# Attention and two expert layers on one core: the order of all instructions taken from a list schedule written in the source

## The chip, the core and the metric

The kernel runs on one core of a Trainium2 chip. A core has a matrix engine (TensorE, PE in the profile), a vector engine (VectorE, DVE), an activation engine (ScalarE, ACT), a general engine (GpSimd, POOL), and a queue on SyncE (SP) from which this kernel starts all its DMA transfers. Each engine issues its own instructions in a fixed order. Semaphores order them across engines. The metric is the device time of one execution in microseconds (us), the median of several.

## What is computed

The reference, cut to what matters (B, H, S, D = 4, 8, 576, 64; 2304 tokens):

```
scores = q @ k.T / sqrt(D)          # heads 0-3: local mask of 32, heads 4-7: strided mask of 32
x = softmax(scores) @ v             # (2304, 512)
h = x @ w_in                        # 512 -> 2048
g = (a0 + a1 h + a2 h^2 + a3 h^3) / (1 + |b0||h| + |b1|h^2 + 1e-6)
x = g @ w_out                       # 2048 -> 512
h = x @ w_in2                       # 512 -> 1024
u = h * softmax(h); ln = (u - mean) / sqrt(var + 1e-6) * g_ln
out = ln @ w_out2                   # 1024 -> 512
```

## The kernel before

All large products are made with three f16 matmuls, from a high and a low f16 part of each operand. The weights arrive as 64-bit words, so each is converted first: `w_conv` unpacks 1024 columns of words with three VectorE instructions (L151 to L153) and squares them on ScalarE (L159), `w_scales` adds the squares over partitions on TensorE (L84) and makes a power-of-two scale, and `w_split` writes the high part on ScalarE (L184) and the low part on VectorE (L185). `w_in` ("wi") and `w_out` ("wo") have eight granules each. `w_in2` and `w_out2` are converted later, in `w2_work`, with the parts made on ScalarE and GpSimd (L212 to L214).

Attention is cut into 12 units for each of the four batches: scores into a PSUM bank (L291, L292), maximum (L318), exponential (L334), normalisation on GpSimd (L343), transposition on TensorE (L353), product with v (L383), and two evacuations into the f16 blocks `xs` (L414, L422).

The expert layers run over nine blocks of 256 tokens. A block has eight groups of 256 hidden columns, and a step n handles one group: `mm_h` (24 matmuls, L535 to L537) fills one of two "h" banks, five steps later `mm_y` (24 matmuls, L612 to L614) consumes the group's result. Between them a group takes ScalarE (L543, L546, L569, L574, L596), GpSimd (L552, L556, L600) and VectorE (L560, L564, L578, L582, L586). The "h" bank is held until L586, since the reciprocal is written back into it. From step 24 on the second expert layer follows, one tile of 128 tokens for each four steps: `mm_in2` (L645 to L647), its softmax and norm, two transposing DMAs (L713, L714), `mm_out2` (L723 to L725) and `out_evac` (L730).

Order before: the source traces every operation with a priority (`prio`, `p_step`), and the framework's scheduler, which simulates a timeline, picks the order in which each engine issues and which buffer of a ring a tile gets. Attention of batch 0 has the priorities 1000 to 6500, all eight `w_conv("wi")` and their splits 10000 to 12100, step n `40000 + 2000 n`, the "wo" granules those of steps 0 to 7, the `w2_work` of step n those of step n + 2.

Of the kernel before, what the change touches and what calls it, by code (L numbers as in the profile page):

```python
# [7 lines left out]

F32 = mybir.dt.float32
F16 = mybir.dt.float16  # L10
BF16 = mybir.dt.bfloat16
# [25 lines left out]
EXPM = 0x7F800000  # L37


@with_exitstack  # L40
def kernel(ctx: ExitStack, tc: tile.TileContext, qk, v, w_in, w_out, ab, w_in2, w_out2, gln, out):
    nc = tc.nc
    PE, ACT, DVE, POOL, SP = nc.tensor, nc.scalar, nc.vector, nc.gpsimd, nc.sync

    const = ctx.enter_context(tc.tile_pool(name="const", bufs=1))
    wts = ctx.enter_context(tc.tile_pool(name="wts", bufs=1))
    big = ctx.enter_context(tc.tile_pool(name="big", bufs=1))
    tiny = ctx.enter_context(tc.tile_pool(name="tiny", bufs=2))
    ps = ctx.enter_context(tc.tile_pool(name="ps", bufs=1, space=PSUM))

    wi_h = wts.tile([128, KD, DFF], F16, name="wi_h")
# [18 lines left out]
    gs_t = const.tile([128, KF2], F32, name="gs_t")  # L70
    gm2 = const.tile([128, 1], F32, name="gm2")

    def psum(tag, shape=(128, 512), bufs=1):
        return ps.tile(list(shape), F32, tag=tag, name=f"ps_{tag}", bufs=bufs)

    def t1(name, n=1, bufs=2):
        return tiny.tile([128, n], F32, tag=name, name=name, bufs=bufs)

    def ew(name, bufs, shape=(128, 512), dt=F32):
        return big.tile(list(shape), dt, tag=name, name=name, bufs=bufs)  # L80

    def sum_over_partitions(x):
        t = psum("a", bufs=2)[:, 0:x.shape[1]]
# [79 lines left out]
    def w_scales(name, g0, n):  # L163
        sg = sum_over_partitions(ssq[name][:, g0:g0 + n])
        p, s = pat[name][:, g0:g0 + n], scl[name][:, g0:g0 + n]
        DVE.tensor_scalar(p.bitcast(I32), sg.bitcast(I32), 1, EXPM, op0=ALU.logical_shift_right, op1=ALU.bitwise_and)
        DVE.tensor_scalar(s.bitcast(I32), p.bitcast(I32), -1.0, float(EXPM - (51 << 23)), op0=ALU.mult, op1=ALU.add)
# [74 lines left out]
        qk_t[b, p] = t  # L242

    def load_vl(b):
        t = big.tile([128, NLB, 4, D], F32, tag="vl", name="vl", bufs=1)
        SP.dma_start(out=t, in_=v[b, :, 0:NLB])
        vl_t[b] = t

    def load_vs(b):
        t = big.tile([128, NSG, 4, D], F32, tag="vs", name="vs", bufs=1)  # L250
        SP.dma_start(out=t, in_=v[b, :, NLB:NVB])
        vs_t[b] = t

# [182 lines left out]
    def x_scale(i):  # L436
        key = k = blk_key(i)
        if key not in xkey:
            m = vmax[key]
            p = const.tile([128, 1], F32, name=f"xp{k}")  # L440
            s = const.tile([128, 1], F32, name=f"xsc{k}")
            mg = t1("mg")
            DVE.tensor_scalar(mg, m, 2.0 ** -60, None, op0=ALU.add)
            pow2(mg, p, s, 13)
            xkey[key] = (m, p, s)
        xm[i], xpw[i], xsc[i] = xkey[key]
        xs[i] = big.tile([128, 2, KD, TB], F16, tag="xs", name="xs", bufs=4)

    def x_tail(b):
        i = ((b + 1) * S - 1) // TB  # L450
# [280 lines left out]
        SP.dma_start(out=out[t * 128:(t + 1) * 128, :], in_=ot)  # L731


    def prio(p):
        tc.cur_priority = p

    LY = 5
    NSTEP = NB * NG
    M2S = 24
    NT2 = NT // 128  # L740
    P_STEP = 2000
    P0 = 40000

    def p_step(n):
        return P0 + int(n * P_STEP)

    prio(0)
    for t in qk_buf:
        qk_zero(t)
    load_qk(0, 0)  # L750
# [10 lines left out]
    for g in range(3, 8):  # L761
        w_load("wi", g)

    make_identity(nc, ident)
    DVE.memset(ones_f, 1.0)
    for t in sm_buf:
        POOL.memset(t, 1e-9)
# [11 lines left out]
    POOL.tensor_copy(mask_b[0:LQ, 0, 0:LW], mask_l0)  # L779
    POOL.tensor_copy(mask_b[0:LQ, 1, 0:LW], mask_l)  # L780
    POOL.tensor_copy(mask_b[0:126, 2, 0:126].rearrange("p (r t) -> p r t", t=TPR), mask_s)
    ACT.preload_act_table_set("natural_log_exp_and_others")
    ACT.activation(aba, ab_t, AF.Abs)

    v_max(0)
    x_scale(0)
    x_scale(1)
    for u in range(12):
        prio(1000 + 500 * u)
        attn_scores2(0, u)  # L790
        attn_softmax(0, u)
        attn_exp(0, u)
        attn_norm(0, u)
        attn_tp(0, u, "a")
        attn_tpe(0, u)
        attn_pv(0, u, "a")
        attn_xhi(0, u)
        attn_xlo(0, u)
    for g in range(8):
        prio(10000 + 300 * g)  # L800
        w_conv("wi", g)
    for g0 in range(0, 8, 2):
        prio(10000 + 300 * g0)
        w_scales("wi", g0, 2)
        for g in range(g0, g0 + 2):
            prio(10000 + 300 * g)
            w_split("wi", g)
    prio(900)
    w_pmax("wi")
    g_scale(0)  # L810
    gsc[1] = gsc[0]
    prio(20000)
    for g in range(4):
        w_load("wo", g)
    load_qk(1, 0)
# [21 lines left out]
    def step(n):  # L837
        if n == 49:
            x_scale(NB - 1)
            g_scale(NB - 1)  # L840
            x_tail(B - 1)
        un, up, upp = units.get(n), units.get(n - 1), units.get(n - 2)
        hg, h1, h2, hm, hy = grp(n), grp(n - 1), grp(n - 2), grp(n - 3), grp(n - LY)
        if un and un[1] == 0:
            b = un[0]
            v_max(b)
            for j in range((b * S) // TB, ((b + 1) * S - 1) // TB):
                x_scale(j)
                g_scale(j)
            x_tail(b - 1)  # L850
        m = n - M2S
        t, sub = divmod(m, 4) if m >= 0 else (-9, 0)
        t_in = t if 0 <= t < NT2 else None
        t_pr = t - 1 if 0 <= t - 1 < NT2 else None
        t_out = t - 2 if 0 <= t - 2 < NT2 else None

        do(un, attn_scores1, *(un or ()))
        do(t_in is not None and sub == 2, m_max, t_in)
        do(upp, attn_xhi, *(upp or ()))
        do(h2, a_ln, *(h2 or ()))  # L860
        do(t_in is not None and sub == 2, m_exp, t_in)
        do(h2, a_ex, *(h2 or ()))
        do(h1, a_abs, *(h1 or ()))
        do(upp, attn_xlo, *(upp or ()))
        do(h1, v_q1, *(h1 or ()))
        do(h2, v_t, *(h2 or ()))
        do(h1, v_p2, *(h1 or ()))
        do(h2, v_rn, *(h2 or ()))
        do(h1, v_p3, *(h1 or ()))
        do(h2, v_g, *(h2 or ()))  # L870
        do(h1, p_qm, *(h1 or ()))
        do(un, attn_softmax, *(un or ()))
        if hy:
            mm_y(*hy, 0)
            mm_y(*hy, 1)
        do(hg, mm_h, *(hg or ()))
        do(up, attn_tp, *(up + ("a",) if up else ()))
        if sub < 2 and t_in is not None:
            if n >= NSTEP + LY:
                prio(p_step(n - 4))  # L880
            mm_in2(t_in, sub)
            prio(p_step(n + 0.5))
        if sub >= 2 and t_out is not None:
            mm_out2(t_out, sub - 2)
        do(up, attn_tpe, *(up or ()))
        do(up, attn_pv, *(up + ("a",) if up else ()))
        do(hm, a_hi, *(hm or ()))
        do(hm, p_lo, *(hm or ()))
        do(un, attn_exp, *(un or ()))
        if t_in is not None and sub == 2:  # L890
            m_u(t_in)
        if t_in is not None and sub == 3:
            m_sq(t_in)
            m_var(t_in)
            m_rs(t_in)
        if t_pr is not None and sub == 0:
            m_nw(t_pr)
            m_v(t_pr)
            m_hi(t_pr)
        if t_pr is not None and sub == 1:  # L900
            m_lo(t_pr)
        do(un, attn_norm, *(un or ()))
        if hy and hy[1] == NG - 1:
            y_scale(hy[0])
            y_evac(hy[0])
            y_evac2(hy[0])
        if t_out is not None and sub == 3:
            out_evac(t_out)
        if un:
            b, u = un  # L910
            if u == 3:
                load_qk(b, 2)
            if u == 6:
                load_qk(b, 3)
            if b < B - 1:
                if u == 7:
                    load_vl(b + 1)
                if u == 9:
                    load_qk(b + 1, 0)
                if u == 11:  # L920
                    load_qk(b + 1, 1)
        if up and up[1] == 11 and up[0] < B - 1:
            load_vs(up[0] + 1)

    def wo_work(g):
        w_conv("wo", g)
        if g + 4 < 8:
            w_load("wo", g + 4)
        if g % 2 == 2 - 1:
            w_scales("wo", g + 1 - 2, 2)  # L930
            for j in range(g + 1 - 2, g + 1):
                prio(p_step(j))
                w_split("wo", j)
        if g == 7:
            w_pmax("wo")
            for j in range(2):
                sl = slice(64 * j, 64 * j + 64)
                POOL.tensor_copy(cwo[sl, :], inv["wo"][sl, j::2])
# [18 lines left out]
    for n in range(M2S + 4 * (NT2 + 2)):  # L957
        if 0 <= n < 4:
            for g in (2 * n, 2 * n + 1):
                prio(p_step(g))  # L960
                wo_work(g)
        prio(p_step(n + 2))
        w2_work(n)
        prio(p_step(n))
        if n >= M2S and (n - M2S) % 8 == 0 and (n - M2S) // 8 < NB:
            y_scale2((n - M2S) // 8)
        step(n)


def _layout(q, k, v):  # L970
# [53 lines left out]
```

## Time and profile before

| what | value |
|---|---|
| timed executions | 793.4, 796.77, 797.81 us; median 796.77 us |
| span of the profiled execution, first to last instruction | 790.5 us |
| what lies around the span, against the median | 6.3 us |
| TensorE busy | 705.6 us (89%), mean granted clock 0.935 |
| VectorE, ScalarE, GpSimd busy | 570.7, 481.6, 329.0 us |
| chain that ended last | TensorE 70%, VectorE 14%, DMA 5%, ScalarE 5% |

The profile is a separate execution from the three timed ones, and its own time is known only as its span. A granted clock of 1.00 is TensorE's upper level. Records of matmuls overlap: the starts of successive ones tell their pace.

### The profile page before, as it was taken

The numbers are of one execution on the slowest core, as the hardware profiler recorded it, in microseconds if no ns is written. First come the engines' busy times: TensorE is split into PE (matmuls) and PEld (weight loads), VectorE is DVE, ScalarE is ACT, GpSimd is POOL, SyncE is SP. The second block draws the span as 40 slices with busy tenths as digits, with TensorE's granted clock in tenths as the row PEclk, the third lists the DMA queues.
The fourth block names the chain that finished last, engine by engine and source line by source line (L and its number), as shares of the span: only waits on it lengthen the run. The fifth ranks groups of instructions, "written<-read, shape, count | busy, mean of one in ns | idle before, by whom it ended". The sixth has DMA issues, their size and how long they took to land.

```text
span 790.5 us, 14385 instructions
## 1 busy us (share of the span) xinstructions
PE 705.6 (89%) x5406; PEld 534.3 (68%) x5406; DVE 570.7 (72%) x1194; ACT 481.6 (61%) x1143; POOL 329.0 (42%) x312
## 2 busy tenths in 40 slices
PE   4777226999987798999999999999999999999997
PEld 4665115887874687687878786777777777766443
DVE  4889999778869875787977575866657657654562
ACT  2776547766784777876766676746556556543442
POOL 2322425646467547754544434434343434330000
PEclk8665557999999999999999999999999999999999
DMA  9994700153231411122111201011022010111134
GB/s 256 321 257 141 196 18 1 33 161 103 72 102 55 138 34 41 33 54 66 33 41 33 41 2 41 2 41 41 1 41 39 4 41 16 25 41 40 41 80 106
DMA packets 68100, 55.97 MB, mean 71 GB/s; under 512 B 39616, under 2 KB 56000, under 8 KB 67520
## 3 DMA queue, kind: packets, MB, share of 16 engines
q1 hardware_dynamic: 68032, 55.07, 26.8%
q8 instruction: 42, 0.69, 0.4%
q14 instruction: 26, 0.21, 0.1%
HBM read 40.90 MB, written 4.72 MB: 58 GB/s over the span
## 4 chain that ended last, share of the span: by engine, by line
PE 70%; DVE 14%; DMA 5%; ACT 5%; issue 4%; POOL 2%; SPq 1%; ACTq 0%; DVEq 0%; POOLq 0%
PE ps_h L535 7%; PE ps_y L613 7%; PE ps_y L614 7%; PE ps_y L612 7%; PE ps_h L537 7%; PE ps_h L536 7%; PE ps_h L647 3%; PE ps_h L646 3%; PE ps_h L645 3%; PE ps_a L292 3%; PE ps_a L725 3%; PE ps_a L723 3%; PE ps_a L724 3%; PE ps_a L383 3%; DMA wi_h<-in_w_in_dram 2%
## 5 line engine op out<-in xcount | busy, mean ns | idle before, releaser
L535 PE MATMUL ps_h<-xs,wi_h 128*128 128x256 f16 x576 | 161.1, 280 | 25.9 <-DVE p L586 25.8
L536 PE MATMUL ps_h<-xs,wi_h 128*128 128x256 f16 x576 | 161.0, 279 | 0.0
L537 PE MATMUL ps_h<-xs,wi_l 128*128 128x256 f16 x576 | 160.5, 279 | 0.0
L613 PE MATMUL ps_y<-gtb,wo_h 128*128 128x256 f16 x448 | 122.2, 273 | 0.7 <-POOL gtb L600 0.7
L612 PE MATMUL ps_y<-gtb,wo_h 128*128 128x256 f16 x448 | 122.2, 273 | 0.6 <-DVE ysb L628 0.6
L614 PE MATMUL ps_y<-gtb,wo_l 128*128 128x256 f16 x448 | 122.2, 273 | 0.0
L600 POOL TENSOR_TENSOR gtb<-p,gtb 128x512 f16<-128x512 f32 x56 | 66.0, 1178 | 119.5 <-ACT gtb L596 119.5
L552 POOL TENSOR_SCALAR q<-A,aba 128x512 f32<-128x512 f32 x72 | 62.7, 870 | 105.3 <-ACT A L543 105.1
L556 POOL TENSOR_TENSOR q<-q,A 128x512 f32<-128x512 f32 x72 | 99.1, 1377 | 5.3
L560 DVE TENSOR_TENSOR p<-p,ps_h 128x512 f32<-128x512 f32 x72 | 49.2, 683 | 48.3 <-ACT p L546 46.3
L569 ACT ACTIVATE L<-q 128x512 f32<-128x512 f32 x72 | 45.4, 630 | 63.4 <-POOL q L556 63.2
L578 DVE SCALAR_TENSOR_TENSOR q<-q,ps_h 128x512 f32<-128x512 f32 x72 | 49.0, 681 | 41.7 <-ACT ps_h L574 41.2
L535 PEld LDWEIGHTS <-wi_h 128*128 128x128 f16 x576 | 58.0, 101 | 31.0 <-DVE p L586 21.9
L543 ACT ACTIVATE A<-ps_h,ih 128x512 f32<-128x512 f32 x72 | 49.1, 682 | 35.0 <-PE ps_h L537 35.0
L536 PEld LDWEIGHTS <-wi_h 128*128 128x128 f16 x576 | 57.7, 100 | 14.3 <-issue 5.8
L343 POOL TENSOR_TENSOR e<-e,arc 96x508 f32<-96x508 f32 (+3 forms) x36 | 38.9, 1081 | 62.6 <-DVE arc L342 41.6
L612 PEld LDWEIGHTS <-wo_h 128*128 128x128 f16 x576 | 56.5, 98 | 11.1 <-DVE ysb L628 0.9
L537 PEld LDWEIGHTS <-wi_l 128*128 128x128 f16 x576 | 57.7, 100 | 8.2
L613 PEld LDWEIGHTS <-wo_h 128*128 128x128 f16 x576 | 56.5, 98 | 9.9 <-issue 0.2
L596 ACT ACTIVATE gtb<-p 128x512 f16<-128x512 f32 x56 | 35.5, 633 | 44.2 <-DVE p L586 44.1
L614 PEld LDWEIGHTS <-wo_l 128*128 128x128 f16 x576 | 56.4, 98 | 7.6 <-issue 1.0
L334 ACT ACTIVATE e<-ps_a,amx 96x127 f32<-96x127 f32 (+2 forms) x132 | 45.6, 358 | 17.4 <-DVE amx L318 13.7
(331 smaller groups left out, 1811.7 us busy)
## 6 DMA issues: line engine op xcount, KB each, us to landing
qkb<-in_qk_dram SPq DMA_DIRECT2D x28, 304.0 KB, 4.6
out_dram<-ot SPq DMA_DIRECT2D x18, 256.0 KB, 2.5
wo_l<-in_w_out_dram SPq DMA_DIRECT2D x4, 1024.0 KB, 5.7
wo_h<-in_w_out_dram SPq DMA_DIRECT2D x4, 1024.0 KB, 5.4
vl<-in_v_dram SPq DMA_DIRECT2D x4, 768.0 KB, 5.9
wi_h<-in_w_in_dram SPq DMA_DIRECT2D x3, 1024.0 KB, 6.7
wi_l<-in_w_in_dram SPq DMA_DIRECT2D x3, 1024.0 KB, 6.6
wo_h<-in_w_in_dram SPq DMA_DIRECT2D x3, 1024.0 KB, 18.2
```

Of the source, the lines that this page charges most:

```text
L535: PE.matmul(o, lhsT=wi_h[:, k, f:f + 128], rhs=xs[i][:, 0, k, :], start=(k == 0), stop=False)
L536: PE.matmul(o, lhsT=wi_h[:, k, f:f + 128], rhs=xs[i][:, 1, k, :], start=False, stop=False)
L537: PE.matmul(o, lhsT=wi_l[:, k, f:f + 128], rhs=xs[i][:, 0, k, :], start=False, stop=(k == KD - 1))
L543: ACT.activation(A, t, AF.Abs, scale=gsc[i]["ih"][:, g:g + 1])
L552: POOL.tensor_scalar(w["q"], w["A"], aba[:, 5:6], aba[:, 4:5], op0=ALU.mult, op1=ALU.add)
L556: POOL.tensor_tensor(w["q"], w["q"], w["A"], op=ALU.mult)
L560: DVE.tensor_tensor(w["p"], w["p"], hp[i, g], op=ALU.mult)
L578: DVE.scalar_tensor_tensor(w["q"], w["q"], EPS_D, w["r"], op0=ALU.add, op1=ALU.mult)
L600: POOL.tensor_tensor(t[:, :, 1, :], gw.pop((i, g))["p"].rearrange("p (c t) -> p c t", t=TB), t[:, :, 0, :], op=ALU.subtract)
L612: PE.matmul(o, lhsT=wo_h[:, f, w], rhs=gg[:, c, 0, :], start=(f == 0 and d % 2 == 0), stop=False, skip_group_check=True)
L613: PE.matmul(o, lhsT=wo_h[:, f, w], rhs=gg[:, c, 1, :], start=False, stop=False, skip_group_check=True)
L614: PE.matmul(o, lhsT=wo_l[:, f, w], rhs=gg[:, c, 0, :], start=False, stop=(f == KF - 1), skip_group_check=True)
```

## The change

Every call on an engine is recorded first (`Order.record`), with its inputs and outputs as regions of fixed buffers, instead of being traced into the framework. The rings of buffers keep their sizes (two "h" banks, two "a" banks, one pair for "y", one for "h2", two T, one ws, and so on), but which one a value gets is chosen by the list schedule, and the values of a ring are given buffers strictly in the order of the source. Small one-column tiles rotate over six places instead of two. `Order.run` estimates the duration of each instruction, works out due times backward from the last one, and places one instruction after another: of those that can begin within 0.2 us of the earliest, the one that is due first. `Order.emit` issues them in that order in a block in which the framework adds semaphores but does not reorder. The priorities go. "wi" is converted in pairs: conversion, scales and split of granules 0 and 1 stand in the source before attention unit 4, the next pairs before units 6, 8 and 10.

```diff
+    def cost(self, op):
...
+        if op.eng == "PE":
+            f32 = op.ins[-1][1].dtype == F32
+            op.t = max(0.03, size(out) / 2400 * ((3.6 if op.call == "transpose" or out.shape[0] > 64 else 1.8) if f32 else 1))
+        elif op.eng == "ACT":
+            op.t = 0.08 + n * 0.00088 + (0.05 if psum else 0) + (0.09 if "accum_out" in op.k else 0)
...
+        elif op.eng == "DVE":
...
+            fast = not two and not psum and op.call == "tensor_scalar"
+            op.t = 0.07 + n / (1900 if fast else 960) + (0.08 if "accum_out" in op.k else 0)
...
+            op.port = n >= 8 and (len(sb) >= 2 if two else fast)
+        elif op.eng == "POOL":
...
+            op.t = 0.1 + n * (0.002 if h else 0.0022 if two else 0.00125 if op.call == "tensor_scalar" else 0.001)
...
+            op.port = bool(ins)
...
+    def run(self):
...
+        LAG = dict(PE=0.25, ACT=0.15, DVE=0.13, POOL=0.1, SP=0.0)
+        EARLY, PEARLY = 0.3, 1.5
...
+        def begin(op):
+            x = max(free[op.eng], op.ready)
+            if op.port:
+                x = max(x, port)
+            for v in op.values:
+                if v.home is None:
+                    f = [max(cells.get(c, 0.0) for c in h) for h, _ in v.homes]
+                    x = max(x, min(f)) if v.queue[0] is v else BUSY
+            return x
...
+                t, d, i = min((x for x in c if x[0] <= t + SLACK), key=lambda x: x[1:])
...
+            if op.eng == "PE":
+                heat = min(3.4, max(0.0, heat - max(0.0, t - free["PE"])) + d)
+                warm = heat > 3.3 or warm and heat > 1.5
+                d = d if warm else 2 * d
...
+                o.ready = max(o.ready, end + (0.0 if o.eng == op.eng == "PE" else 0.06 if o.eng == op.eng else LAG[op.eng] + (PEARLY if o.eng == "PE" else EARLY)))
...
     def ew(name, bufs, shape=(128, 512), dt=F32):
-        return big.tile(list(shape), dt, tag=name, name=name, bufs=bufs)
+        return View(Value(rings[name], shape, dt))
...
+    def wi_pair(g0):
+        for g in range(g0, g0 + 2):
+            w_conv("wi", g)
+        w_scales("wi", g0, 2)
+        for g in range(g0, g0 + 2):
+            w_split("wi", g)
+
     for u in range(12):
-        prio(1000 + 500 * u)
+        if u in (4, 6, 8, 10):
+            wi_pair(u - 4)
...
-    for g in range(8):
-        prio(10000 + 300 * g)
-        w_conv("wi", g)
...
-            if n >= NSTEP + LY:
-                prio(p_step(n - 4))
             mm_in2(t_in, sub)
-            prio(p_step(n + 0.5))
...
         step(n)
+    order.emit(order.run())
```

## Rows read from the trace of the kernel before

**Rows 1.** The page's part 1: busy us (share of the span) and instructions.
```profile
PE 705.6 (89%) x5406; PEld 534.3 (68%) x5406; DVE 570.7 (72%) x1194; ACT 481.6 (61%) x1143; POOL 329.0 (42%) x312
```
**Rows 2.** The page's part 2: busy tenths in 40 slices of 19.8 us.
```profile
PE   4777226999987798999999999999999999999997
...
DVE  4889999778869875787977575866657657654562
...
PEclk8665557999999999999999999999999999999999
```
**Rows 3.** Busy time by stage: stage, length, busy us (instructions) by engine, granted clock.
```profile
core 0: us, PE busy (x) PEld busy (x) DVE busy (x) ACT busy (x) POOL busy (x), PEclk, DMA share, GB/s
0.00:20.00 20.00, 8.89 (x46) 8.29 (x47) 9.96 (x16) 5.61 (x20) 5.49 (x23) 0.85 0.91 255
20.00:79.00 59.00, 44.55 (x277) 36.41 (x276) 52.24 (x122) 41.91 (x138) 17.30 (x12) 0.65 0.84 240
79.00:140.00 61.00, 24.10 (x160) 19.07 (x159) 59.85 (x122) 35.34 (x67) 25.23 (x17) 0.64 0.28 71
140.00:330.00 190.00, 171.71 (x1527) 143.95 (x1525) 145.67 (x307) 133.61 (x352) 117.99 (x107) 0.97 0.26 80
330.00:740.00 410.00, 409.87 (x3192) 305.92 (x3191) 279.22 (x575) 245.56 (x535) 163.00 (x155) 1.00 0.15 32
740.00:790.50 50.50, 46.46 (x215) 20.70 (x213) 23.76 (x57) 19.56 (x34) 0.00 (x0) 1.00 0.37 83
```
**Rows 4.** TensorE's waits in the whole span: total us, times, longest.
```profile
PE ps_h L535 <- DVE p L586: 25.8, 6, 14.0
PE ps_a L84 <- ACT wo_h L159: 15.7, 1, 15.7
PE ps_a L353 <- DVE xs L422: 7.4, 5, 3.3
```
**Rows 5.** VectorE's waits from 0 to 79 us, same columns.
```profile
DVE vam L256 <- DMA vl<-in_v_dram: 6.4, 1, 6.4
DVE T L151 <- DMA wi_h<-in_w_in_dram: 2.5, 1, 2.5
```
**Rows 6.** Busy time of two stretches of 10 us, columns as in rows 3.
```profile
240.00:250.00 10.00, 5.42 (x19) 1.99 (x18) 10.00 (x28) 6.06 (x22) 6.10 (x4) 0.83 0.30 105
260.00:270.00 10.00, 5.92 (x54) 4.78 (x54) 9.03 (x24) 5.65 (x16) 5.00 (x5) 0.99 0.29 70
```
**Rows 7.** VectorE's busy time from 0 to 140 us on L151, L152, L153.
```profile
0.00:140.00 140.00, 12.64 (x16) 0.67 0.61 168
...
0.00:140.00 140.00, 20.32 (x16) 0.67 0.61 168
...
0.00:140.00 140.00, 20.05 (x16) 0.67 0.61 168
```
**Rows 8.** Timeline of VectorE: start us, us, instruction [idle before].
```profile
83.62 1.23 DVE L485 TENSOR_TENSOR ih<-ih,ih 128x8 f32<-128x8 f32 x1
...
234.46 2.61 DVE L151 TENSOR_SCALAR T<-wo_h 128x1024 int32<-128x1024 int32 x1
...
248.73 0.12 DVE L485 TENSOR_TENSOR ih<-ih,ih 128x8 f32<-128x8 f32 x1
...
262.62 0.68 DVE L151 TENSOR_SCALAR T<-wo_l 128x1024 int32<-128x1024 int32 x1
...
269.66 0.73 DVE L318 TENSOR_REDUCE amx<-ps_a 96x2 f32<-96x254 f32 x2
270.32 1.20 DVE L153 SCALAR_TENSOR_TENSOR T<-wo_l,T 128x1024 int32<-128x1024 int32 x1
```
**Rows 9.** Timeline of GpSimd from 234 us.
```profile
234.38 2.14 POOL L214 TENSOR_TENSOR wi_l<-ws,wi_h 128x1024 f16<-128x1024 f32 x1
236.47 2.58 POOL L214 TENSOR_TENSOR wi_l<-T,wi_h 128x1024 f16<-128x1024 f32 x1
```
**Rows 10.** The page's part 5: line, operation, count | busy us, mean ns | idle before.
```profile
L552 POOL TENSOR_SCALAR q<-A,aba 128x512 f32<-128x512 f32 x72 | 62.7, 870 | 105.3 <-ACT A L543 105.1
L556 POOL TENSOR_TENSOR q<-q,A 128x512 f32<-128x512 f32 x72 | 99.1, 1377 | 5.3
L560 DVE TENSOR_TENSOR p<-p,ps_h 128x512 f32<-128x512 f32 x72 | 49.2, 683 | 48.3 <-ACT p L546 46.3
```

More of the change, by code (lines that the diff above doesn't have):

```diff
@@ L6 @@
 from concourse._compat import with_exitstack
-from concourse.masks import make_identity
 F32 = mybir.dt.float32
@@ L37, with _tensor, __init__, at @@
 EXPM = 0x7F800000
+def _tensor(x):
+    return getattr(x, "tensor", None) is not None and type(x.tensor).__name__ == "Tile"
+class Value:
+    def __init__(self, homes, shape, dt):
+        self.homes, self.shape, self.dt = homes, shape, dt
+        self.home, self.left, self.base = None, 0, {}
+    def at(self, j):
+        if j not in self.base:
+            _, t = self.homes[j]
+            n = 1
+            for x in self.shape[1:]:
+                n *= x
+            if self.dt != F32:
+                t = t.bitcast(self.dt)
+            t = t[0:self.shape[0], 0:n]
+            if len(self.shape) == 3:
+                t = t.rearrange("p (a b) -> p a b", b=self.shape[2])
+            elif len(self.shape) == 4:
+                t = t.rearrange("p (a b c) -> p a b c", b=self.shape[2], c=self.shape[3])
+            self.base[j] = t
+        return self.base[j]
@@ new lines, with __init__, at, more @@
+class View:
+    def __init__(self, value, ops=()):
+        self.value, self.ops, self.seen = value, ops, {}
+    def at(self, j):
+        if j not in self.seen:
+            x = self.value.at(j)
+            for name, a, k in self.ops:
+                x = getattr(x, name)(*a, **k)
+            self.seen[j] = x
+        return self.seen[j]
+    def more(self, name, *a, **k):
+        return View(self.value, self.ops + ((name, a, k),))
+    def __getitem__(self, k):
+        return self.more("__getitem__", k)
+    def rearrange(self, *a, **k):
+        return self.more("rearrange", *a, **k)
+    def bitcast(self, dt):
+        return self.more("bitcast", dt)
+    def unsqueeze(self, d):
+        return self.more("unsqueeze", d)
+    def to_broadcast(self, s):
+        return self.more("to_broadcast", s)
+    @property
+    def shape(self):
+        return self.at(0).shape
@@ L42 @@
     nc = tc.nc
-    PE, ACT, DVE, POOL, SP = nc.tensor, nc.scalar, nc.vector, nc.gpsimd, nc.sync
+    order = Order(tc, dict(PE=nc.tensor, ACT=nc.scalar, DVE=nc.vector, POOL=nc.gpsimd, SP=nc.sync))
+    PE, ACT, DVE, POOL, SP = (order.engine(x) for x in ("PE", "ACT", "DVE", "POOL", "SP"))
     const = ctx.enter_context(tc.tile_pool(name="const", bufs=1))
@@ L47 @@
     big = ctx.enter_context(tc.tile_pool(name="big", bufs=1))
-    tiny = ctx.enter_context(tc.tile_pool(name="tiny", bufs=2))
     ps = ctx.enter_context(tc.tile_pool(name="ps", bufs=1, space=PSUM))
@@ L71 @@
     gm2 = const.tile([128, 1], F32, name="gm2")
+    singles = [ps.tile([128, 512], F32, name=f"bank{j}") for j in range(4)]
+    pairs = [ps.tile([128, 1024], F32, name=f"banks{j}") for j in (4, 6)]
+    banks = {
+        "h": [((("bank", j),), singles[j]) for j in (0, 1)],
+        "a": [((("bank", j),), singles[j]) for j in (2, 3)],
+        "y": [((("bank", 4), ("bank", 5)), pairs[0])],
+        "h2": [((("bank", 6), ("bank", 7)), pairs[1])],
+    }
+    WORDS = dict(e=(2, 512), p=(3, 512), q=(2, 512), A=(1, 512), L=(1, 512), pts=(1, 512), T=(2, 1024), ws=(1, 2048), ot=(1, 512), tail=(1, 1024), xs=(4, 1024), vl=(1, 1536), vs=(1, 1280))
+    rings = {k: [(((k, j),), big.tile([128, w], F32, name=f"{k}{j}")) for j in range(n)] for k, (n, w) in WORDS.items()}
     def psum(tag, shape=(128, 512), bufs=1):
-        return ps.tile(list(shape), F32, tag=tag, name=f"ps_{tag}", bufs=bufs)
+        return View(Value(banks[tag], shape, F32))
     def t1(name, n=1, bufs=2):
-        return tiny.tile([128, n], F32, tag=name, name=name, bufs=bufs)
+        at = small.setdefault(name, [])
+        if len(at) < 6:
+            at.append(tiny[:, sum(small_n):sum(small_n) + n])
+            small_n.append(n)
+        else:
+            at.append(at.pop(0))
+        return at[-1]
+    small, small_n = {}, []
+    tiny = const.tile([128, 512], F32, name="tiny")
     def ew(name, bufs, shape=(128, 512), dt=F32):
-        return big.tile(list(shape), dt, tag=name, name=name, bufs=bufs)
+        return View(Value(rings[name], shape, dt))
     def sum_over_partitions(x):
@@ L244, in load_vl @@
     def load_vl(b):
-        t = big.tile([128, NLB, 4, D], F32, tag="vl", name="vl", bufs=1)
+        t = ew("vl", 1, (128, NLB, 4, D))
         SP.dma_start(out=t, in_=v[b, :, 0:NLB])
@@ L249, in load_vs @@
     def load_vs(b):
-        t = big.tile([128, NSG, 4, D], F32, tag="vs", name="vs", bufs=1)
+        t = ew("vs", 1, (128, NSG, 4, D))
         SP.dma_start(out=t, in_=v[b, :, NLB:NVB])
@@ L446, in x_scale @@
         xm[i], xpw[i], xsc[i] = xkey[key]
-        xs[i] = big.tile([128, 2, KD, TB], F16, tag="xs", name="xs", bufs=4)
+        xs[i] = ew("xs", 4, (128, 2, KD, TB), F16)
     def x_tail(b):
@@ L731, in out_evac @@
         SP.dma_start(out=out[t * 128:(t + 1) * 128, :], in_=ot)
-    def prio(p):
-        tc.cur_priority = p
     LY = 5
@@ L740 @@
     NT2 = NT // 128
[L741 to L747, printed above, removed]
     for t in qk_buf:
@@ L762 @@
         w_load("wi", g)
-    make_identity(nc, ident)
+    POOL.memset(ident, 0.0)
+    POOL.affine_select(ident, ident, pattern=[[-1, 128]], compare_op=ALU.not_equal, fill=1.0, base=0, channel_multiplier=1)
     DVE.memset(ones_f, 1.0)
@@ L781 @@
     POOL.tensor_copy(mask_b[0:126, 2, 0:126].rearrange("p (r t) -> p r t", t=TPR), mask_s)
-    ACT.preload_act_table_set("natural_log_exp_and_others")
+    nc.scalar.preload_act_table_set("natural_log_exp_and_others")
     ACT.activation(aba, ab_t, AF.Abs)
@@ L798 @@
         attn_xlo(0, u)
-    for g in range(8):
-        prio(10000 + 300 * g)
-        w_conv("wi", g)
[L802 to L808, printed above, removed]
     w_pmax("wi")
@@ L811 @@
     gsc[1] = gsc[0]
-    prio(20000)
     for g in range(4):
@@ L931, in wo_work @@
             for j in range(g + 1 - 2, g + 1):
-                prio(p_step(j))
                 w_split("wo", j)
@@ L959 @@
             for g in (2 * n, 2 * n + 1):
-                prio(p_step(g))
                 wo_work(g)
-        prio(p_step(n + 2))
         w2_work(n)
-        prio(p_step(n))
         if n >= M2S and (n - M2S) % 8 == 0 and (n - M2S) // 8 < NB:
```

186 lines of the change are left out of this document (added).

## Prediction

> **What bounds the kernel now.** I read the totals first, then the slices, then one table by stage, and only then waits. The totals [rows 1] name TensorE: 705.6 of 790.5 us. They hide that this is an average over stages with different limits. In the slices [rows 2] TensorE stands at 2 tenths in slices 4 and 5 (79 to 119 us) under a low clock, and at 9 almost everywhere from slice 7 on. The table by stage [rows 3] gives the limits:
>
> - 0 to 20 us: the first loads. VectorE is idle for 10.0 us, of which 6.4 and 2.5 are waits for v and for the first weight [rows 5].
> - 20 to 79 us, attention of batch 0 and the conversion of wi: VectorE 52.24 of 59, so 6.8 us idle.
> - 79 to 140 us, the rest of wi's splits, wo's conversion and the first groups: VectorE 59.85 of 61, TensorE 24.10. VectorE sets the end here. TensorE's two longest single waits, 15.7 us for wo's squares and 14.0 us for an "h" bank [rows 4], lie here, but an instruction of VectorE stands behind each of them, so a TensorE that waited less would finish nothing sooner.
> - 140 to 330 us: TensorE 171.71 of 190, clock 0.97. Idle 18.3 us. The clock costs about 0.03 x 171.7 = 5 us more.
> - 330 to 740 us: TensorE 409.87 of 410. Nothing to be had.
> - 740 us to the end: TensorE idle for 4.0 us, a chain of dependent instructions after the last matmuls of the second layer.
>
> So what another order can give back lies in VectorE's gaps and slow instructions before 140 us, and in TensorE's gaps from 140 to 330 us.
>
> **The change, part by part.** The work is the same: no matmul, activation or DMA is added or dropped (the identity matrix is made by two GpSimd instructions in either version). The number and size of the buffers in every ring stay. What changes is the order on each queue, and with it who waits.
>
> *Start, 0 to 20 us.* The same loads, in nearly the same source order, issued by the same queue. The idle time here is waiting for data [rows 5]. I take 0.
>
> *VectorE's idle time, 20 to 79 us: 6.8 us.* It ran dry while attention's short chains passed through the other engines. The list schedule fills such moments with whatever can begin within 0.2 us, and it has conversions to fill with, as before did. Bounds: 6.8 us gained, or as much again lost if the estimates are poor. I take half, 3.4 us gained.
>
> *VectorE's slow instructions before 140 us.* The 48 unpacking instructions L151 to L153 take 12.64 + 20.32 + 20.05 = 53.0 us [rows 7]. Undisturbed ones take 0.68 (L151) and 1.20 (L153, and L152 the same) [rows 8], so 16 x 0.68 + 32 x 1.20 = 49.3 us, and 3.7 us were waiting. An 8-column instruction that takes 0.12 us undisturbed took 1.23 [rows 8]; two of these lines have two such calls each here, for which I add 2 us. That is 5.7 us. What they wait for is seen in the later conversion: L151 took 2.61 us at 234.46 while GpSimd's L214 ran from 234.38 to 236.52, and ended 0.55 us after it [rows 8, 9]. The list schedule has this as a shared port (`op.port`) and tries to place such instructions apart. Bounds 0 and 5.7; half, 2.8 us. [...]
>
> *wi in pairs.* Conversion, scales and split of a pair follow each other, so a pair's staging buffers come free while attention still runs, and wo's loads can start earlier. What waited for wo's loads is about 1 us of VectorE in all, part of it in the 6.8 above. The steps still can't start before attention is done (their x blocks need all units) and before all eight granules are scaled (the group constants need the largest scale). VectorE's sum before the first `mm_y` is the same. I take 0.3 us. So pairing by itself is not a gain. If the cover were gone, an attention chain late behind a pair's 2 x 4.5 us of conversion, the loss would be some 5 us.
>
> *140 to 330 us: 18.3 us idle and 5 us of clock, 23.3 us.* Two stretches show what happens: at 240 to 250 us TensorE is busy 5.42 and VectorE 10.00, with the clock down to 0.83; at 260 to 270 us 5.92 and 9.03 [rows 6]. VectorE is full there because w_in2's and w_out2's conversion, with instructions of 2 to 3 us beside GpSimd [rows 8, 9], came together with a group's five instructions and attention, and `mm_h` found no free "h" bank. Over the stage VectorE is at 145.67 of 190, 77% [rows 3], so the same work fits if it is spread. Due times do that: a conversion of w_in2 is due only before `mm_in2` at step 24, so a group's instruction that is ready goes first; and TensorE's inputs are wanted 1.5 us early. Bounds: 0 and 23.3 us gained. Nearest row for what a good order reaches: 330 to 740 us, with VectorE at 68% and nothing lost. But the conversions can't be spread at will: w_in2's staging lies in buffers that hold parked groups until `mm_y` of block 0 is done. I take 60%, 14 us.
>
> *330 to 740 us.* TensorE is saturated, so order can only lose here. The schedule's estimates are near the measured paces: 512 columns on VectorE come to 0.60 us, beside 0.68 measured with its overlap [rows 10]; GpSimd's L552 and L556 to 0.74 and 1.23 us beside 0.87 and 1.38, 0.28 us short for a group. That is less than the 1.5 us by which TensorE's inputs are early. I take 0.
>
> *The tail: 4.0 us idle.* Its chain is the same, its last tile is placed by due times instead of a priority. 0.5 us gained; bounds -2 and 2.
>
> Sum: 3.4 + 2.8 + 0.3 + 14 + 0.5 = 21 us. The span goes from 790.5 to 769.5; with the 6.3 us around it, 775.8, so 776 us against 796.8, 2.6% less.
>
> **The rivals.**
>
> *All of it comes back (about 759 us).* 6.8 + 5.7 + 0.3 + 23.3 + 2 = 38 us. For it: VectorE has room on average. Against it: full recovery needs every estimate right.
>
> *The "h" banks stay the limit (about 783 us).* `mm_h` waited 25.8 us for L586, 11.8 of it apart from the one long wait [rows 4], and there are two "h" banks as before. If these 11.8 us are a matter of buffers and not of order, the stage from 140 to 330 us gives 60% of 11.5, 7 us, and the sum is 14 us. For it: the waits name that bank. Against it: at 330 to 740 us the same two banks never stop TensorE. [...]
>
> *No change (793 to 800 us).* VectorE is the limit before 140 us whatever the order, and the gaps from 140 to 330 us move instead of going. For it: 59.85 of 61 us. Against it: 77% in the later stage. The order that is issued is the recorded one, so that the change doesn't take effect at all I give no chance of its own.
>
> *Slower: buffers in strict source order (about 812 us).* Before, a tile that was ready could take a free bank. Now scores, transposes, products with v, sums for scales and `mm_out2` take the two "a" banks in the order of the source, and a value whose turn hasn't come waits with its bank free; behind it TensorE's in-order queue waits. The price: a wait of that bank's kind, TensorE's L353 for L422, took 7.4 / 5 = 1.5 us [rows 4]; 36 units of batches 1 to 3, two thirds of them hit, 24 x 1.5 = 36 us more, against 21 gained: 812 us. It decides from 21 / 36 = 0.6 us for each unit on. For it: two banks serve five uses, and `mm_out2` holds one for two steps. Against it: the source's order within a step is also the order of need, and at 330 to 740 us two banks sufficed.
>
> **How the numbers follow.** Chances: the forecast 55% (763 to 789 us), everything back 8%, banks 13%, no change 10%, slower 14%. A measurement of this kernel tells from no change what is over about 0.5%, 4 us. Faster is then 0.55 + 0.08 + 0.13 = 0.76, same 0.10, slower 0.14. The range runs from 757 us, just under the case in which all comes back, to 800 us, the upper end of no change; left out are most of the slower case and the lowest values, together under 2 in 10.
>
> **What would show it.** In the profile of the changed kernel: VectorE over 95% from 20 us until TensorE is full, and TensorE full from about 133 us instead of 140; no 10 us stretch after that with TensorE under 8 us; L151's longest call under 1.5 us; the stage of 410 us with TensorE at 100% as before. It is wrong if TensorE waits on an "a" bank in the steady stage, if VectorE before 140 us shows new idle time, or if TensorE fills much earlier than 130 us, which by my sum VectorE's work forbids.

## The result and the profile after

The changed kernel takes 772.71 us in the median of four executions (771.49 to 773.43), the kernel before 795.14 us beside it on the same chip. The ratio is 0.973, with a 95% interval of 0.967 to 0.978. The forecast was 776 us, a ratio of 0.974. The medians differ by 22.4 us, the two profiled spans by 18.9 us (790.5 and 771.6): executions of the kernel before scatter, and its profiled one was among the shorter.

In the changed kernel every call is issued from one helper, so all instructions have the line L341, and one-column tiles are views of one tile `tiny`. Groups are told apart by tiles. The page's totals and slices after, beside [rows 1, 2]:

```profile
PE 712.6 (92%) x5406; PEld 540.0 (70%) x5406; DVE 592.0 (77%) x1194; ACT 481.8 (62%) x1143; POOL 328.6 (43%) x312
...
PE   3985667999998998999999999999999999999996
...
DVE  6789999989999999798976677666666766744562
...
PEclk9555567999999999999999999999999999999999
```

Busy time by stage after, in the stretches and columns of [rows 3]:

```profile
0.00:20.00 20.00, 7.80 (x40) 6.77 (x41) 12.47 (x24) 5.86 (x20) 6.73 (x24) 0.97 0.94 277
20.00:79.00 59.00, 44.91 (x242) 36.36 (x242) 52.35 (x105) 40.67 (x133) 15.23 (x11) 0.50 0.89 240
79.00:140.00 61.00, 42.64 (x279) 33.84 (x279) 58.92 (x126) 41.26 (x95) 24.44 (x17) 0.66 0.28 73
140.00:330.00 190.00, 182.53 (x1650) 154.22 (x1649) 177.52 (x361) 147.73 (x388) 123.07 (x118) 0.99 0.26 80
330.00:740.00 410.00, 409.74 (x3095) 298.32 (x3094) 278.40 (x554) 234.81 (x491) 159.11 (x143) 1.00 0.16 34
```

Busy time says little here, since a matmul at a low granted clock is busy for longer (in the kernel before, 256 columns for 0.42 us at a clock of 0.50, from 113 to 116 us, and for 0.27 us at 1.00, from 116.5 to 118 us; successive ones start 0.21 and 0.11 us apart there). The count of matmuls says how far TensorE has come. Up to 140 us it has started 479 before and 558 after:

```profile
0.00:140.00 140.00, 77.54 (x479) 63.77 (x480) 122.05 (x258) 82.86 (x224) 48.02 (x52) 0.67 0.61 168
```
```profile
0.00:140.00 140.00, 95.35 (x558) 76.97 (x559) 123.75 (x253) 87.80 (x246) 46.40 (x52) 0.63 0.63 172
```

(The first row is before, the second after.) At 0.109 us, the distance of successive matmuls of 256 columns at a clock of 1.00, these 79 are 8.6 us. From 140 to 330 us it is 1650 against 1527, another 123 or 13.4 us. Together 22.0 us are gained by 330 us, and little after it until the tail. The first figure is a little high: only 35 of the 79 are of 256 columns, and attention's masks and products with v start only 0.04 to 0.06 us apart at that clock (medians by shape behind 330 us, in both traces; its scores 0.12 to 0.14 us). With each shape counted at its own median distance of starts in these two traces, an estimate, the lead is 7 to 8 us at 140 us and 21.4 us at 330 us. How the lead goes on can be read from ScalarE's evacuations of the output. That of the tenth of 18 tiles, and the last, before:

```profile
700.70 0.69 ACT L730 ACTIVATE ot<-ps_a,ic_wo 128x512 f32<-128x512 f32 x1 [0.71 <-PE ps_a L725]
...
786.91 0.69 ACT L730 ACTIVATE ot<-ps_a,ic_wo 128x512 f32<-128x512 f32 x1 [5.03 <-PE ps_a L725]
```

and the same two after:

```profile
677.71 0.69 ACT L341 ACTIVATE ot<-bank,ic_wo 128x512 f32<-128x512 f32 x1 [0.72 <-PE bank L341]
...
768.08 0.69 ACT L341 ACTIVATE ot<-bank,ic_wo 128x512 f32<-128x512 f32 x1 [4.54 <-PE bank L341]
```

The lead is 23.0 us at the tenth tile of 18 and 18.8 us at the last: the tail gave 4.2 us back. TensorE's idle time there is new, and it waits for the transposing DMAs:

```profile
755.09 0.39 PE L341 MATMUL bank<-wo_h,T 128*128 128x512 f16 x1 [2.16 <-DMA T<-ws]
756.55 1.03 PE L341 MATMUL bank<-wo_h,T 128*128 128x512 f16 x2 [0.86 <-DMA T<-ws]
```

TensorE's waits for an "h" bank held by L586 fell from 25.8 us [rows 4] to 9.4, with the same two banks. Most of that is the one long wait of 14.0 us before 140 us. In the stage from 140 to 330 us they fell from 9.8 to 5.8 us. First the whole span after, then that stage before and after:

```profile
PE bank L341 <- DVE p L341: 9.4, 5, 3.6
```
```profile
PE ps_h L535 <- DVE p L586: 9.8, 4, 3.2
```
```profile
PE bank L341 <- DVE p L341: 5.8, 4, 1.8
```

### The profile page after: what moved, and what is told of

The parts are those of the page before. It is cut to its first block, busy times and chain, and to the rows that moved or that the text cites. A ratio compares the mean times of both kernels' runs of the same rounds, so it can differ in the third digit from the quotient of the medians.

```text
span 771.6 us, 14358 instructions
## 1 busy us (share of the span) xinstructions
PE 712.6 (92%) x5406; PEld 540.0 (70%) x5406; DVE 592.0 (77%) x1194; ACT 481.8 (62%) x1143; POOL 328.6 (43%) x312
## 4 chain that ended last, share of the span: by engine, by line
PE 71%; DVE 17%; DMA 4%; issue 4%; ACT 3%; SPq 0%; POOL 0%; ACTq 0%; DVEq 0%
PE bank L341 39%; PE banks L341 32%; DVE p L341 3%; DVE tiny L341 3%; DMA qkb<-in_qk_dram 2%; DVE T L341 2%; DVE gtb L341 2%; DMA vs<-in_v_dram 1%; DVE ws L341 1%; DVE bank L341 1%; DVE xs L341 1%; DVE q L341 1%; DVE wi_l L341 1%; ACT p L341 1%; DVE ysb L341 1%
## 5 line engine op out<-in xcount | busy, mean ns | idle before, releaser
L341 PE MATMUL bank<-xs,wi_h 128*128 128x256 f16 x1152 | 203.5, 281 | 13.4 <-DVE p L341 9.4
L341 PE MATMUL bank<-xs,wi_l 128*128 128x256 f16 x576 | 161.5, 280 | 2.3 <-DVE wi_l L341 2.3
L341 PE MATMUL banks<-gtb,wo_h 128*128 128x256 f16 x896 | 152.1, 273 | 0.1
L341 POOL TENSOR_SCALAR q<-A,aba 128x512 f32<-128x512 f32 x72 | 65.0, 902 | 181.4 <-ACT A L341 181.3
L341 PEld LDWEIGHTS <-wi_h 128*128 128x128 f16 x1152 | 115.7, 101 | 29.6 <-issue 13.4
L341 PEld LDWEIGHTS <-wo_h 128*128 128x128 f16 x1152 | 112.4, 98 | 21.9 <-issue 0.8
L341 PE MATMUL banks<-gtb,wo_l 128*128 128x256 f16 x448 | 122.0, 273 | 0.0
L341 DVE SCALAR_TENSOR_TENSOR p<-p,ac,bank 128x512 f32<-128x512 f32 x144 | 107.5, 747 | 4.7
L341 ACT ACTIVATE A<-bank,ih 128x512 f32<-128x512 f32 x72 | 49.4, 686 | 79.4 <-PE bank L341 79.1
L341 POOL TENSOR_TENSOR q<-q,A 128x512 f32<-128x512 f32 x72 | 91.6, 1272 | 5.5
L341 PE MATMUL banks<-wi_h,ysb 128*128 128x512 f16 x288 | 91.1, 379 | 0.0
L341 PE MATMUL bank<-wo_h,T 128*128 128x512 f16 x272 | 86.3, 383 | 3.0 <-DMA T<-ws 3.0
L341 DVE TENSOR_TENSOR p<-p,bank 128x512 f32<-128x512 f32 x72 | 49.1, 682 | 50.2 <-ACT p L341 49.7
L341 POOL TENSOR_TENSOR gtb<-p,gtb 128x512 f16<-128x512 f32 x56 | 73.5, 1315 | 25.2 <-ACT gtb L341 25.0
L341 PEld LDWEIGHTS <-T 128*128 128x128 f16 x408 | 40.1, 99 | 47.7 <-DMA T<-ws 4.0
L341 PEld LDWEIGHTS <-ysb 128*128 128x128 f16 x432 | 42.2, 98 | 44.0
L341 DVE SCALAR_TENSOR_TENSOR q<-q,bank 128x512 f32<-128x512 f32 x72 | 49.1, 682 | 24.6 <-ACT bank L341 18.7
L341 PEld LDWEIGHTS <-wi_l 128*128 128x128 f16 x576 | 58.1, 101 | 12.3 <-DVE wi_l L341 2.4
L341 POOL TENSOR_TENSOR e<-e,tiny 96x508 f32<-96x508 f32 (+3 forms) x36 | 35.6, 989 | 72.1 <-DVE tiny L341 32.3
L341 ACT ACTIVATE L<-q 128x512 f32<-128x512 f32 x72 | 45.3, 629 | 26.1 <-POOL q L341 26.1
L341 PEld LDWEIGHTS <-wo_l 128*128 128x128 f16 x576 | 56.5, 98 | 6.4
L341 ACT ACTIVATE e<-bank,tiny 96x127 f32<-96x127 f32 (+2 forms) x132 | 45.8, 356 | 20.4 <-DVE tiny L341 15.9
```

The source lines that it names most:

```text
L341: getattr(self.real[op.eng], op.call)(*[real(x) for x in op.a], **{k: real(x) for k, x in op.k.items()})
```

## The experiments

All medians below are of four executions unless said; "changed" is the kernel after, 772.71 us. A difference in matmuls started, times 0.109 us, is called TensorE's lead or lag; it is rough, since it counts all shapes alike.

**e1, wi unpaired.**

```diff
     for u in range(12):
-        if u in (4, 6, 8, 10):
-            wi_pair(u - 4)
         attn_scores2(0, u)
...
+    for g in range(8):
+        w_conv("wi", g)
+    for g0 in range(0, 8, 2):
+        w_scales("wi", g0, 2)
+        for g in range(g0, g0 + 2):
+            w_split("wi", g)
     w_pmax("wi")
```

> The changed kernel with the eight granules of wi recorded after the twelve attention units again (all conversions, then scales and splits), as before. If the pairing carries the gain before 140 us (7.6 us of TensorE work ahead at 140 us), the time goes to about 780 us. If it is the order in general, since VectorE's sum before the first product with wo is the same, it stays at 770 to 776 us.

Measured: 782.05 us, 9.3 above changed. By 140 us it has started 489 matmuls, 69 fewer, a lag of 7.5 us. Taken alone this says that the pairs carry the early gain. e8 to e12 put that in doubt.

**e2, no shared port in the model.**

```diff
             x = max(free[op.eng], op.ready)
-            if op.port:
-                x = max(x, port)
```

> The changed kernel without the shared port in the list schedule's model (begin times ignore it); the rest is the same. If keeping VectorE and GpSimd apart gave part of the gain, time rises by 3 us or more, to 776 us and above, and the unpacking instructions take longer. If the term does not separate them on the chip (before 330 us the changed kernel has no fewer such waits than the kernel before), the time stays within 3 us of 772.7.

Measured: 785.72 us, 13.0 above. The 72 unpacking instructions take 94.0 us in all (55.8 before 140 us and 38.2 after it) against 83.0 in the changed kernel (51.5 and 31.5) and 84.9 in the kernel before. That the changed kernel's waits are hardly fewer than before's had spoken for a term that does little. The right comparison is with the same list without the term, and there it saves 11 us of VectorE. Most of the time is lost after 140 us: the lag is 24 matmuls, 2.6 us, by 140 us, and another 87, 9.5 us, by 330 us.

**e3, the source's index in place of the due time.**

```diff
-                t, d, i = min((x for x in c if x[0] <= t + SLACK), key=lambda x: x[1:])
+                t, d, i = min((x for x in c if x[0] <= t + SLACK), key=lambda x: x[2])
```

> The changed kernel in which, of the instructions that can begin within 0.2 us, the one that stands first in the source is taken instead of the one that is due first. If due times make the stage from 140 to 330 us (conversions of the second layer's weights behind the groups' instructions), TensorE loses 10 to 20 us there again: 783 to 793 us. If placing by begin time alone does it, 772 to 776 us.

Measured: 794.38 us (ten executions), a ratio of 0.999 to the kernel before (0.996 to 1.003): the whole gain is gone.

```profile
0.00:140.00 140.00, 83.74 (x506) 67.61 (x507) 121.84 (x261) 82.47 (x229) 38.30 (x50) 0.65 0.61 172
140.00:330.00 190.00, 175.77 (x1554) 149.47 (x1554) 161.33 (x328) 146.86 (x380) 125.43 (x113) 0.95 0.26 80
```

The lag is 5.7 us by 140 us and 10.5 us more by 330 us, where VectorE is at 161.33 instead of 177.52: with the same work to do it waits again. This list schedule by begin times alone is no better than the framework's.

**e4, the tail.** The kernel before gave `mm_in2` of the last tiles an earlier priority; the changed kernel has them in plain source order.

```diff
-        if sub < 2 and t_in is not None:
+        if sub < 2 and t_in is not None and t_in < TE:
             mm_in2(t_in, sub)
+        te, sube = divmod(n + 4 - M2S, 4) if n + 4 >= M2S else (-9, 0)
+        if sube < 2 and TE <= te < NT2:
+            mm_in2(te, sube)
...
+    TE = 15
```

> The changed kernel with the first products of the second layer of the last three tiles (15 to 17) recorded four steps earlier, as the priority of the kernel before had it. If the 4 us that the changed kernel loses after 700 us come from these products standing too late behind the second products, the time falls by 3 to 5 us, to 768 to 770 us. If the last tile's chain sets the end whatever stands before it, it stays at 772 to 774 us.

Measured: 768.90 us, 3.8 below changed, a ratio of 0.969 to before (0.965 to 0.972). From the tenth tile's evacuation to the last one it takes 763.66 - 676.70 = 87.0 us; changed takes 90.4, before 86.2.

```profile
676.70 0.69 ACT L341 ACTIVATE ot<-bank,ic_wo 128x512 f32<-128x512 f32 x1 [0.71 <-PE bank L341]
...
763.66 0.69 ACT L341 ACTIVATE ot<-bank,ic_wo 128x512 f32<-128x512 f32 x1 [4.91 <-PE bank L341]
```

This is the fastest version of the study.

**e5 and e6, less work for VectorE.** One of three unpacking instructions is left out, for wo alone (e5; the weights lose their signs) or for the second layer's weights alone (e6). The edit of e5:

```diff
-        DVE.scalar_tensor_tensor(Ti, hi, -0x40000000, Ti, op0=ALU.bitwise_and, op1=ALU.bitwise_or)
+        if name != "wo":
+            DVE.scalar_tensor_tensor(Ti, hi, -0x40000000, Ti, op0=ALU.bitwise_and, op1=ALU.bitwise_or)
```

> The changed kernel with one of the three unpacking instructions left out for each of the eight granules of wo (the weights lose their signs), which takes 8 x 1.2 = 9.6 us from VectorE before 140 us. If VectorE's work sets when TensorE fills, the time falls by 8 to 10 us, to 763 to 765 us. If chains or loads set it, by less than 4 us.

> The changed kernel with the same instruction left out for the eight pieces of the second layer's two weights, 8 x 1.2 us and more of VectorE between 140 and 330 us. If TensorE is the limit there by now (7.5 us idle in 190), the time falls by 7 us at most, 766 to 771 us. If VectorE (177.5 busy of 190) still sets the pace, by 9 to 15 us, to 758 to 764 us.

Measured: 764.81 and 768.49 us, 7.9 and 4.2 below changed. The first two rows are e5's, the last two e6's:

```profile
0.00:140.00 140.00, 97.47 (x627) 79.92 (x628) 122.36 (x278) 91.20 (x260) 50.24 (x59) 0.70 0.64 173
140.00:330.00 190.00, 183.91 (x1671) 155.88 (x1669) 177.54 (x342) 150.33 (x388) 128.27 (x117) 1.00 0.29 87
```
```profile
0.00:140.00 140.00, 94.80 (x563) 76.58 (x564) 124.08 (x254) 87.81 (x246) 46.76 (x53) 0.65 0.63 172
140.00:330.00 190.00, 184.75 (x1681) 157.10 (x1680) 174.00 (x360) 151.52 (x397) 124.94 (x121) 0.99 0.29 85
```

In e5 the lead of 69 matmuls, 7.5 us, is there at 140 us and grows by 21 more, 2.3 us, until 330 us: most of the 9.6 us taken from VectorE comes out of the time, as it would where VectorE sets when TensorE fills. In e6 the lead of 31 matmuls, 3.4 us, arises after 140 us: less than half of the 9.6 us comes out, which speaks for TensorE as the closer limit there by now. Both differences are smaller than what a change without an argument can do (e10 below), so each supports its case and does not prove it.

**e7, the list in source order.**

```diff
-            for e, xs in avail.items():
...
+            for i in sorted(i for xs in avail.values() for i in xs):
+                t = begin(ops[i])
+                if t < BUSY:
+                    best = (t, i)
+                    break
```

> The changed kernel's recording, buffers and wi pairs, but instructions placed in the order of the source wherever a buffer allows it, without begin times and due times. If fixed buffers and recording give nothing by themselves and the list schedule is the whole gain, this is far slower, 830 us or more. If the order of the source is nearly as good, 775 to 800 us.

Measured: 1254.12 us. TensorE is busy for 813.0 of 1252 us at a mean clock of 0.817. With the same recording and fixed buffers it is 458 us slower than the kernel before, so the gain is not theirs: it comes from the order in which the list places the instructions. This edit drops the begin times and the due times together.

```profile
PE 813.0 (65%) x5406; PEld 590.4 (47%) x5406; DVE 569.7 (45%) x1194; ACT 483.3 (39%) x1143; POOL 303.9 (24%) x312
```

**e8, pairs alone, in the kernel before.** `wi_pair` of the diff, called before units 4, 6, 8 and 10 after `prio(1000 + 500 * u)`, in place of the loops over `w_conv("wi", g)` and its splits.

> The kernel before with only the pairs of wi put in (conversion, scales, splits of two granules before units 4, 6, 8 and 10, at those units' priorities), framework's scheduler and priorities otherwise as before. If the pairs are worth something by themselves, it falls by 4 to 8 us. If VectorE's sum decides, it stays within 4 us of the kernel before.

Measured: 807.67 us beside 796.04 for before, a ratio of 1.015 (1.011 to 1.019): slower by 11.6 us, which neither case had.

```profile
0.00:140.00 140.00, 82.93 (x464) 67.16 (x465) 118.57 (x255) 81.72 (x230) 44.75 (x50) 0.62 0.63 172
140.00:330.00 190.00, 163.51 (x1438) 136.72 (x1436) 144.88 (x288) 122.88 (x323) 105.02 (x98) 0.95 0.24 74
```

Only 15 matmuls of the lag, 1.6 us, are there at 140 us, where the pairs stand. The other 89, 9.7 us, come in the stage after it, in which this edit moves nothing in the source. So it seems that an early edit reshuffled a later stage; how is not shown.

**e9, e10, e11: controls.** e1, e2 and e8 could be such reshuffles. So three constants without an argument were changed on the kernel of e4: `SLACK = 0.25` instead of 0.2, `EARLY = 0.35` instead of 0.3, and TensorE's `/ 2400` as `/ 2350`.

> A control for e1 and e2: the kernel of e4 with a constant of the list schedule changed that nobody argues for (instructions within 0.25 us of the earliest compete, not 0.2 us). If the list is robust, so that the 9 and 13 us of e1 and e2 are their edits' own, the time stays within 3 us of 768.9. If any small change of the list moves it by as much, it lands 6 us or more away.

> The second control on the kernel of e4: inputs are wanted 0.35 us early instead of 0.3 us. Robust: within 3 us of 768.9. Any change moves it: 6 us or more away.

> The third control on the kernel of e4: the estimate of TensorE's pace 2% slower (0.109 us for 256 columns, as the trace has it, instead of 0.107 us). Robust: within 3 us of 768.9. Any change moves it: 6 us or more away. If a better estimate helps, below 766 us.

Measured: 770.46, 779.43 and 774.25 us, 1.6, 10.5 and 5.4 above e4. They ran on another chip than e4; by the ratios to the kernel before beside each (0.970, 0.981 and 0.974 against 0.969) it is 0.6, 10 and 4 us, much the same. The list is not robust: a constant that moves by 0.05 us costs up to 10.5 us. Up to 140 us e4, e9 and e10 have started 566, 511 and 493 matmuls:

```profile
0.00:140.00 140.00, 95.08 (x566) 76.79 (x567) 124.47 (x255) 87.91 (x246) 46.91 (x53) 0.65 0.62 172
```
```profile
0.00:140.00 140.00, 80.71 (x511) 64.62 (x512) 120.73 (x242) 83.80 (x232) 45.09 (x52) 0.71 0.63 172
```
```profile
0.00:140.00 140.00, 83.25 (x493) 66.55 (x493) 122.53 (x243) 81.82 (x228) 47.30 (x51) 0.67 0.63 172
```

So e10's loss sits mostly before 140 us (8.0 us), the same place as e1's. But e9 lags there by 55 matmuls, 6.0 us, too, and wins more than half of it back by 330 us (1680 against 1651 in that stage): a lag at 140 us is not yet lost time. The better estimate of the pace did not help. All three leave the unpacking instructions near where they were (85.3, 85.5 and 85.4 us), and so do e1, e3 and e12 (85.3, 82.1 and 84.7 us), so e2's 94.0 us are the port term's own, while its 13.0 us are not all proven to be.

**e12, unpaired under another constant.** e1's edit on the kernel of e9.

> The kernel of e9 with wi unpaired as in e1. If the pairs themselves carry 9 us in a list schedule, as e1 against the changed kernel says, this is 778 to 782 us, 8 us or more above e9's 770.5. If e1 was one more of the changes that move the list by chance, as the controls e9 to e11 suggest (1.6, 10.5 and 5.4 us for edits without an argument), it lies within 4 us of 770.5 or below it.

Measured: 774.30 us, 3.8 above e9, where e1 was 9.3 above changed: within the case of chance by 0.2 us. But e9 and e12 ran on different chips, beside medians of 792.17 and 794.21 us for the kernel before, and by ratio (0.976 against 0.970) the difference is some 5 us, which neither case had. So it decides nothing.

## Why the prediction was right, point by point

**The bound by stage** held as far as the rows go. VectorE is busy for 58.92 of the 61 us before 140 us (and in e5 7.9 of 9.6 us come out), TensorE is full from about 130 us, and nothing moved in the 410 us behind 330 us (409.74 busy).

**The number.** That 776 us fits this well is in part luck. The sum gave 21 us, and the profiled spans fell by 18.9 us, to 771.6 us where 769.5 was forecast. The 6.3 us around the span were wrong the other way: on record every execution of either kernel takes some 1.8 us more than its own span, so the profiled execution before took about 792.3 us, and the other 4.5 us are scatter between executions.

**Before 140 us**: forecast 6.5 us, measured 8.6 by the count of matmuls and 7 to 8 with their shapes, by other terms than I gave. VectorE's idle time from 20 to 79 us did not shrink: 6.65 us against 6.76, where I took 3.4 as gained. The first 20 us, put at nothing, gave 2.5 us: VectorE is busy 12.47 us instead of 9.96, since v's load is issued first, before q and k, and the maximum over it starts at 5.28 instead of 10.00 us.

```profile
5.28 1.75 DVE L341 TENSOR_REDUCE tiny<-vl 128x1 f32<-128x1536 f32 x1 [1.56 <-DMA vl<-in_v_dram]
```

I had the same loads "in nearly the same source order"; due times order them too. The slow unpacking instructions gave 1.7 us (the same 48 take 51.5 us after, 53.2 before, when each is added up whole), and the short ones of L484 and L485 2.5 us: before, four of them took 2.85 us, after, two take 0.3 us and the other two run behind 140 us. That is 4.2 us, where I took 2.8 for both. From 79 to 140 us VectorE stands idle for 0.9 us more than before (58.92 of 61 against 59.85), which I had named as a sign of being wrong; over all 140 us its idle time still fell, from 17.95 to 16.25 us. These rows together are 5.9 us. The last of the 48 unpacking instructions begins 6.0 us earlier:

```profile
121.63 1.63 DVE L153 SCALAR_TENSOR_TENSOR gtb<-wo_l,gtb 128x1024 int32<-128x1024 int32 x1
```
```profile
115.67 1.22 DVE L341 SCALAR_TENSOR_TENSOR gtb<-wo_l,gtb 128x1024 int32<-128x1024 int32 x1
```

**The pairs**, taken at 0.3 us: not settled. Without them the list is slower by 9.3 and 3.8 us, with them the framework's schedule is slower by 11.6, and changes without any argument move a list by 1.6 to 10.5. That they are worth nothing is not shown, nor what they are worth. One reason I gave was too strict: a step can begin before attention is done. The first matmul of an `mm_h` starts at 61.2 us in the changed kernel, against 72.6 before and 74.2 in e1, though the 25th such matmul starts at 88.2 us, against 76.7 before.

**140 to 330 us**: forecast 14, measured 13.4 us. It was right that due times make this gain: without them all is lost (e3, 21.7 us, twice the largest scatter of a control). It was wrong that they do it by spreading the conversions. The 24 unpacking instructions of the second layer begin between 169.4 and 280.1 us before, and between 168.3 and 279 us after. VectorE did not become less full but fuller, 177.52 of 190 us, and in the same stage it does 125 of the groups' instructions instead of 109. What went is its own waiting: 44.3 us idle before, 12.5 after. The two longest waits before, and the longest after:

```profile
DVE q L578 <- ACT ps_h L574: 10.7, 7, 2.7
DVE qkb L241 <- DMA qkb<-in_qk_dram: 10.0, 7, 2.7
```
```profile
DVE tiny L341 <- PE bank L341: 2.5, 7, 0.6
```

Which of the orders that due times change does this, VectorE's, ScalarE's or that of the loads, no run shows.

**The tail**: forecast 0.5 us gained, measured 4.2 lost, beyond the lower bound of -2. This is the step that failed. I wrote that its last tile is placed by due times "instead of a priority" and did not ask what that priority had done. TensorE's due times follow the source's order, in which `mm_in2` of a tile stands behind `mm_out2` of an earlier one that nothing waits for. So the last tile's chain started late, with too little work left to cover it: behind the last `mm_in2`, 48 matmuls of earlier tiles' `mm_out2` are left, where before it was 72, and in e4 it is 72 again. e4 recovers 3.4 of the 4.2 us.

**The rivals.** Buffers in strict source order: TensorE has no wait of that size in the steady stage. The "h" banks as the limit: the time that this rival gives did not come, and in the stage from 140 to 330 us the order alone took 4.0 of that wait's 9.8 us with the same two banks. But the 5.8 us that remain are most of the 7.5 us for which TensorE still stands idle there, and no run has a third bank, so for these it stays open.

**What I said would show**: TensorE full from about 133 us was right (from 130 to 230 us it is busy for 9.31 of every 10 us or more, at a granted clock of 1.00), and so was the longest L151, 1.19 us. "VectorE over 95% from 20 us" was wrong (52.35 of 59 is 89%), and two stretches of 10 us fall just under the 8 us that I gave as a floor:

```profile
240.00:250.00 10.00, 7.84 (x66) 5.85 (x65) 9.82 (x20) 7.61 (x21) 6.26 (x6) 1.00 0.56 210
...
300.00:310.00 10.00, 7.89 (x68) 6.36 (x67) 9.89 (x13) 6.59 (x21) 7.85 (x8) 0.94 0.17 41
```

## What to carry to other kernels

Where several engines take turns as the limit, the order in which an engine works off its instructions can be worth more than instructions saved (21.7 us in e3, 7.9 in e5); what made it here is a due time worked back from the consumer, not the list as such. A hand-written priority that a scheduler replaces should be asked what it did before it goes, and its end effects looked at first: the tail's was worth 4 us. A list schedule's result scatters under meaningless edits, here by 1.6 to 10.5 us, so an edit's own worth can be read only against such controls, and from rows of its own place, not from the total alone.

## What the runs showed of the hardware

- An instruction of VectorE on 8 columns outlasted four of GpSimd's. At 300.10 us a `tensor_scalar` of 8 columns began and took 4.65 us, and it ended 0.03 us after the last of four two-input instructions of GpSimd, which ran back to back from 300.22 to 304.72 us. The same instruction beside an idle GpSimd took 0.22 us. VectorE at 300 us, GpSimd beside it, then VectorE at 148 us:

```profile
300.10 4.65 DVE L341 TENSOR_SCALAR ac<-ih,tiny 128x8 f32<-128x8 f32 x1
```
```profile
299.71 0.55 POOL L341 TENSOR_TENSOR e<-e,tiny 108x216 f32<-108x216 f32 x1 [0.21 <-DVE tiny L341]
300.22 4.50 POOL L341 TENSOR_TENSOR wo_l<-ws,wo_h 128x512 f16<-128x512 f32 x4
```
```profile
148.64 0.22 DVE L341 TENSOR_SCALAR ac<-ih,tiny 128x8 f32<-128x8 f32 x1
```

  At 300.10 us an instruction of GpSimd had been running since 299.71, and VectorE's ended only behind the four that followed it. In the kernel before, the L151 of 234.46 us [rows 8, 9] ended 0.55 us after the first L214, while the second one was running, which began at 236.47 us and took 2.58 us instead of 2.14. Why VectorE's instruction outlasted four of GpSimd's in the one case and one in the other, no run shows.
- From 20 to 79 us the granted clock is 0.50 for the whole stage, with TensorE busy 44.91 of 59 us; before it was 0.65 there [rows 3]. The kernel is faster all the same. VectorE, the fuller engine of that stage with 52.35 of 59 us, waited there for TensorE for 4.1 us, against 4.8 before, so the lower clock shows no cost in it; no run has this order at a clock of 1.00 there. In slices of 0.5 us, the clock of the trace before is 1.00 in 1368, 0.50 in 195 and between the two in 17; of the trace after in 1320, 214 and 8. No slice is above 1.00.
